# A decode block streaming its key and value cache: the query weights as four strided loads on two DMA queues

## The chip, the core and the metric

The kernel runs on one core of one Trainium2 chip. The metric is device time in microseconds (us) of one execution; lower is better. A core has five engines that run side by side, each with its own instruction queue: TensorE (PE) for matrix products, VectorE (DVE) and ScalarE (ACT) for elementwise work and reductions, GpSimd (POOL), and SyncE (SP), which here only issues transfers. Transfers between memory (HBM) and the on-chip SBUF of 128 partitions are done by 16 DMA engines. A transfer is issued by an engine into its own DMA queue: SyncE's transfers appear in the profile as queue q1, ScalarE's as queue q10. Engines and transfers wait for one another through semaphores.

## The reference, cut to what matters

One decoding step (a single new token for each of two sequences) of a transformer block, all in float32: layer norm, attention over a cache of 8192 keys and values for each of 32 heads of 128, and a gated feed-forward block, each with its residual.

```python
def _A_ref(x, k_cache, v_cache, wq, wo):       # x [2,1,512], caches [2,32,8192,128]
    q = (x @ wq).reshape(B, Sq, H, Dh).transpose(0, 2, 1, 3)
    scores = jnp.einsum("bhqd,bhkd->bhqk", q, k_cache) * (Dh ** -0.5)
    p = _softmax(scores, axis=-1)
    o = jnp.einsum("bhqk,bhkd->bhqd", p, v_cache)
    return o.transpose(0, 2, 1, 3).reshape(B, Sq, H * Dh) @ wo

h = x + _A_ref(_layernorm(x), k_cache, v_cache, wq, wo)     # wq [512,4096], wo [4096,512]
g, u = silu(_layernorm(h) @ w_gate), _layernorm(h) @ w_up   # [512,1792] each
out = h + (g * u) @ w_down                                  # w_down [1792,512]
```

The caches are by far the largest part of what is read: 2 x 268 MB of some 565 MB.

## The kernel before, in words

Everything is written out by hand: each engine has its own list of steps (`steps`), `do` appends an instruction that raises a semaphore, `wait` appends a wait for a semaphore to reach a value, and `emit` writes the lists out engine by engine.

**Units.** The attention is cut into U = 32 units, each of one sequence and two neighbouring heads. Keys of a unit fill one slot of 128 partitions by 64 KB (64 partitions per head, 128 keys of 128 numbers in each); there are two slots for keys, `kslot`, used in turn, and one, `vslot`, for values. For each unit VectorE multiplies the keys by the query (L435) and reduces the products to scores (L444), in two halves; TensorE and ScalarE make the softmax weights (L335 to L340, L395 to L401), and TensorE multiplies them with the values (`pe_values`, L345).

**Loads.** `loads` (L146 to L199) is a list in the order in which SyncE issues it (L594 to L597): wq first, then the first unit's keys in two halves, the second unit's keys, and from then on values and keys in turn, then wo, w_gate, w_up and w_down. `after` (L204 to L208) says which loads must wait because their slot is still in use: the first values wait for wq's last use, since wq lies in `vslot` until the query projection is done; the third unit's keys wait for the first unit's scores, and so on. wq, the halves of the first keys and the second unit's keys wait for nothing, so SyncE issues these four one behind another at the start.

Each whole load (wq, keys or values of a unit) is 8.389 MB: 128 rows of 64 KB, one for each partition. For wq a partition p holds the rows 4p to 4p+3 of the matrix, that is the four weights that belong to the features 4p to 4p+3 (L162).

**Start.** ScalarE issues the load of x (4 KB, L211). When it has landed, VectorE and GpSimd normalise it (`layernorm`, L235 to L258, called at L260), TensorE transposes the result (L255), and VectorE copies it into the form of a matmul operand (L289 and L294). TensorE then waits for that operand and for wq (L297) and makes the queries of all units: 8 groups of 16 instructions in the source, 128 matmuls in the trace (L308), each group copied out by ScalarE (L319). VectorE's first multiply waits for the first group's queries and for the first half of the first keys. The end of the last group is what frees `vslot` (`freed["wq", 0]`, L321).

Of the kernel before, what the change touches and what calls it, by code (L numbers as in the profile page):

```python
# [9 lines left out]
P = 128  # L10
# [3 lines left out]
class Program:  # L14
# [16 lines left out]
    def wait(self, engine, *points):  # L31
        for s, value in points:
            if self.known[engine].get(s, 0) < value:
                self.known[engine][s] = value
                self.steps[engine].append(lambda e, s=s, v=value: e.wait_ge(s, v))  # L35

    def do(self, engine, fn, sem=None, by=1):

        if sem is None:
            self.steps[engine].append(fn)  # L40
            return None
        self.count[sem] += by
        self.steps[engine].append(lambda e: fn(e).then_inc(sem, by))
        return sem, self.count[sem]
# [8 lines left out]
def decode_block(nc, x, k_cache, v_cache, wq, wo, w_gate, w_up, w_down, out):  # L53
# [24 lines left out]
    def sbuf(name, *shape, align=32):  # L78
        return nc.alloc_sbuf_tensor(name, list(shape), F32, align_bytes=align).ap()
# [7 lines left out]
    vslot = sbuf("vslot", P, SLOT, align=512)  # L87
# [44 lines left out]
    wait, do = g.wait, g.do  # L132
# [3 lines left out]
    s_dve_pe, s_act_pe, s_v = (g.sem(n) for n in ("dve_pe", "act_pe", "v"))  # L136
    s_k = [g.sem(f"k{n}") for n in range(2)]

    def alone(name):
        return g.sem(name)  # L140
# [3 lines left out]
    landed = {}  # L144
    freed = {}
    loads = []  # L146
# [7 lines left out]
    def load_kv(kind, i, parts=1):  # L154
        cache, t = (k_cache, kslot[i % 2]) if kind == "k" else (v_cache, vslot if i < U - 1 else v_last)
        n = SLOT // parts
        for c in range(parts):
            own = parts > 1 or (kind, i) == ("v", U - 1)
            sem = alone(f"{kind}{i}_{c}") if own else s_k[i % 2] if kind == "k" else s_v
            loads.append(((kind, i), c, t[:, c * n : (c + 1) * n], k_src(cache, i)[:, c * n : (c + 1) * n], sem))  # L160

    loads.append((("wq", 0), 0, vslot, wq.rearrange("(p c) m -> p (c m)", p=P), s_v))  # L162
    load_kv("k", 0, 2)
    for i in range(1, U):
        load_kv("k", i)
# [42 lines left out]
            after["k", i] = ("k", i - 2)  # L208


    do("scalar", lambda e: e.dma_start(xs, x.rearrange("b s d -> (b s) d")), x_in := alone("x"), 16)  # L211
    p0 = do("gpsimd", lambda e: e.memset(ident, 0.0), s_pool)
    wait("gpsimd", p0)
# [21 lines left out]
    def layernorm(src, ready):  # L235
        wait("vector", *ready)
        p = do("vector", lambda e: e.bn_stats(stats, src), s_dve)  # L237
        wait("vector", p)
        p = do("vector", lambda e: e.bn_aggr(mv, stats), s_dve)
        wait("vector", p)  # L240
        p = do("vector", lambda e: e.tensor_scalar(ve, mv[:, 1:2], EPS, None, op0=OP.add), s_dve)
        wait("gpsimd", p)
        p = do("gpsimd", lambda e: e.tensor_tensor(rstd, ve, mhalf, op=OP.pow), s_pool)
        wait("vector", p)
        p = do(
            "vector",
            lambda e: e.tensor_scalar(y, src, mv[:, 0:1], rstd, op0=OP.subtract, op1=OP.mult),
            s_dve,
        )
        normed = p  # L250
        wait("tensor", p, ident_done)
        for c in range(DC):
            p = do(
                "tensor",
                lambda e, c=c: e.transpose(yt[:, c, :], y.rearrange("b (p c) -> b c p", c=DC)[:, c, :], ident[:B, :B]),  # L255
                s_pe if c == DC - 1 else None,
            )
        return normed, p  # L258

    _, p = layernorm(xs, [(x_in, 16)])  # L260


    for t, value in (
# [25 lines left out]
    p = do("vector", lambda e: e.tensor_copy(xT, yt), s_dve)  # L289
    wait("vector", p)  # L290
    xb = osb.rearrange("p (c m) -> p c m", c=DC * B)
    xb_done = do(
        "vector",
        lambda e: e.tensor_copy(xb, xT.rearrange("p c b -> p (c b)")[:, :, None].to_broadcast([P, DC * B, HP])),  # L294
        s_dve,
    )
    wait("tensor", xb_done, landed[("wq", 0), 0])  # L297
    wqv = vslot.rearrange("p (c m k d) -> p c k m d", c=DC, k=2, d=DH)
    q_done = []
    for n, (m, b) in enumerate((m, b) for m in range(0, MQ, 4) for b in range(B)):  # L300
# [3 lines left out]
        for c in range(DC):  # L304
            for k in range(2):
                p = do(
                    "tensor",
                    lambda e, ps=ps, c=c, k=k, m=m, b=b: e.matmul(  # L308
                        ps[HALF[k]],
                        xb[:, c * B + b, :],  # L310
                        wqv[:, c, k, m : m + 4, :],
                        start=(c == 0),
                        stop=(c == DC - 1),
                    ),
# [111 lines left out]
    for i in range(U):  # L426
        m, b = divmod(i, B)
        parts = 2
        n = NJ // parts
        wait("vector", q_done[m // 4 * B + b])  # L430
        for c in range(parts):
# [7 lines left out]
            if i and c == 1:  # L439
                recip(i - 1)  # L440
            wait("vector", mult)
            p = do(
                "vector",
                lambda e, kt=kt, s=scores[i % 2][:, c * n : (c + 1) * n]: e.tensor_reduce(s, kt, axis=AX.X, op=OP.add),  # L444
                s_dve,
            )
        freed["k", i] = p
        if i:
# [16 lines left out]
    p = do(  # L465
        "vector",
        lambda e: e.tensor_tensor(
            om,
            oT.rearrange("p h b -> p b h")[:, :, :, None].to_broadcast([P, B, H, NQ]),
            quarter[:, None, None, :].to_broadcast([P, B, H, NQ]),  # L470
            op=OP.mult,
        ),
        s_dve,
    )
    wait("tensor", p)
    for b in range(B):
        p = do(
            "tensor",
            lambda e, b=b: e.matmul(
                oq_ps[:, b, :], om[:, b].rearrange("p h q -> p (h q)"), fold, start=True, stop=True  # L480
            ),
            s_pe if b == B - 1 else None,
        )
    wait("scalar", p)
    p = do("scalar", lambda e: e.activation(oq.rearrange("p c b -> p b c"), oq_ps, AF.Copy), s_act)
    wait("tensor", p, zeroed)
    for c in range(H):
        for e_, (c0, n) in enumerate(WO):
            if c0 == c:
                wait("tensor", landed[("wo", 0), e_])  # L490
        t = c % 4
        p = do(
            "tensor",
            lambda e, c=c, t=t: e.matmul(
                wide[0][32 * t : 32 * t + B, :],
                oq[:, c, :],
                wo_t[:, c * D : (c + 1) * D],
                start=(c < 4),
                stop=(c >= H - 4),
            ),  # L500
# [4 lines left out]
    p = do("scalar", lambda e: e.activation(osb, wide[0], AF.Copy), s_act)  # L505
# [13 lines left out]
    def project_f(first, ps):  # L519
        for c in range(DC):  # L520
            for e_, (c0, n) in enumerate(WF):
                if c0 == first + c:
                    wait("tensor", landed[("wf", 0), e_])
            w = wf_t[:, (first + c) * F : (first + c + 1) * F]
            for t in range(4):
                p = do(
                    "tensor",
                    lambda e, c=c, t=t, w=w: e.matmul(
                        ps[32 * t : 32 * t + 32, :],
                        hT[:, c, :],  # L530
                        w[:, t * FQ : (t + 1) * FQ],
                        start=(c == 0),
                        stop=(c == DC - 1),
                    ),
                    s_pe if c == DC - 1 and t == 3 else None,
                )
        return p

    gate, up = wide[1][:, :FQ], wide[0][:, :FQ]
    p = project_f(0, gate)  # L540

    wait("tensor", h1_done)
    for t in range(4):
# [8 lines left out]
    p = do("scalar", lambda e: e.activation(sg, gate, AF.Sigmoid), s_act)  # L552
    wait("vector", p)
    sg_done = do("vector", lambda e: e.tensor_mul(sg, gate, sg), s_dve)
    p = project_f(DC, up)
# [4 lines left out]
    p = do(  # L560
        "vector",
        lambda e: e.tensor_mul(
            gu.rearrange("p (c j) -> p j c", c=FB),
            up.rearrange("p (j c) -> p j c", c=FB),
            sg.rearrange("p (j c) -> p j c", c=FB),
        ),
        s_dve,
    )
    gT = rest[:, D + 2 * FQ : D + 3 * FQ]
    wait("vector", p)  # L570
    p = do("vector", lambda e: e.transpose(gT, gu), s_dve)
    wait("tensor", p)
    for c in range(FB):
# [3 lines left out]
        for t in range(4):  # L577
            p = do(
                "tensor",
                lambda e, c=c, t=t: e.matmul(  # L580
                    f_ps[32 * t : 32 * t + 32, :],
                    gT[:, c * 32 : (c + 1) * 32],
                    wd_t[:, c * D + t * P : c * D + (t + 1) * P],
                    start=False,
                    stop=(c == FB - 1),
                ),
# [62 lines left out]
```

## Time and profile before

| what | us |
|---|---|
| median of 3 runs (lowest, highest) | 1309.85 (1309.34, 1310.26) |
| the profiled execution, its own time | 1309.67 |
| its span, from the first instruction to the last | 1308.3 |
| VectorE busy | 1131.1 (86%) |
| TensorE's matmuls busy | 434.5 (33%) |
| DMA, mean over the span | 432 GB/s |

The times that the prediction works with are those of the one profiled execution, which also has some time around its span. The page of the profile gives busy times of each engine, a strip of 40 equal slices with the business of each engine in tenths, the DMA queues with their packets, and groups of instructions. The other views are the chain of work that ended last (followed back from the end, at each step to what released it), the timeline (instructions in order of time, with the idle time before each in square brackets and what ended it), the DMA view for a window (packets, queues, issues with the time from issue to landing) and busy times by window. An engine's name with a q (SPq, ACTq) marks an entry for issuing a transfer. L308 is line 308 of the kernel.

### The profile page before, as it was taken

Reading aid. Unit: us, or ns where it says so; the run is one execution under the profiler, and the core shown is the slowest. Engines: PE = TensorE matmul, PEld = TensorE weight load, DVE = VectorE, ACT = ScalarE, POOL = GpSimd, SP = SyncE. Lnnn points to the kernel's source line nnn. Section 1 sums busy time; section 2 is a strip of 40 time slices with the busy share of each in tenths; the row PEclk is TensorE's granted clock in tenths of the full one; section 3 lists DMA queues with packets and bytes.
Section 4 is the critical chain, followed back from the end, with each engine's and each line's share of the span. In section 5 each row is a group of like instructions: output and inputs, shape, how many; then the busy total and the mean of one; then the engine's idle time right before and its main releaser. Section 6 shows DMA issues by size and latency. Waiting matters only on the chain.

```text
span 1308.3 us, 6707 instructions
## 1 busy us (share of the span) xinstructions
PE 434.5 (33%) x2952; PEld 136.3 (10%) x2952; DVE 1131.1 (86%) x246; ACT 80.4 (6%) x271; POOL 3.1 (0%) x15
## 2 busy tenths in 40 slices
PE   3643223333213333312333321333332233332177
PEld 1210001011001011100101100101100010110022
DVE  0999988899888889988888988888998888898841
ACT  0100000000000000000000000000000000000010
POOL 0000000000000000000000000000000000000000
PEclk9865566666556666656666655666655666665578
DMA  9999999999999999999999999999999999999998
GB/s 404 443 433 439 427 433 435 437 431 439 427 443 423 445 421 445 431 437 437 431 439 427 443 423 445 421 443 431 439 437 427 443 427 439 427 441 425 441 424 371
DMA packets 10969, 564.79 MB, mean 432 GB/s; under 512 B 1222, under 2 KB 1230, under 8 KB 1616
## 3 DMA queue, kind: packets, MB, share of 16 engines
q1 hardware_dynamic: 10944, 564.66, 99.7%
q8 instruction: 5, 0.08, 0.0%
q14 instruction: 4, 0.03, 0.0%
q10 hardware_dynamic: 16, 0.01, 0.0%
HBM read 564.66 MB, written 0.00 MB: 432 GB/s over the span
## 4 chain that ended last, share of the span: by engine, by line
DMA 54%; DVE 45%; PE 1%; SPq 0%; issue 0%; DVEq 0%
DMA kslot<-in_A_k_cache_dram 48%; DVE kslot L435 22%; DVE s L444 22%; DMA kslot<-in_A_v_cache_dram 3%; DMA kslot<-in_B_w_down_dram 3%; PE opart L345 1%; DVE gm L388 0%; SPq L597 0%; DVE r L414 0%; PE bank L580 0%; DVE m L452 0%; DVE kslot L591 0%; DVEq L35 0%
## 5 line engine op out<-in xcount | busy, mean ns | idle before, releaser
L435 DVE TENSOR_TENSOR kslot<-kslot,qsb 128x8192 f32<-128x8192 f32 x64 | 555.6, 8681 | 127.7 <-DMA kslot<-in_A_k_cache_dram 127.7
L444 DVE TENSOR_REDUCE s<-kslot 128x64 f32<-128x8192 f32 x64 | 555.2, 8675 | 0.1
L345 PE MATMUL opart<-vslot,pz 128*8 128x512 f32 x1984 | 285.2, 740 | 246.0 <-DMA vslot<-in_A_v_cache_dram 246.0
L337 PE MATMUL bank<-gm,nscale 1*64 1x1 f32 x64 | 11.8, 250 | 358.4 <-DVE gm L388 358.4
L345 PEld LDWEIGHTS opart<-vslot,pz 128*8 128x8 f32 x1984 | 55.4, 103 | 449.7 <-DMA vslot<-in_A_v_cache_dram 248.7
L335 PE MATMUL bank<-ident,m 128*1 128x128 f32 x64 | 18.7, 395 | 169.3 <-DVE m L452 169.3
L337 PEld LDWEIGHTS bank<-gm,nscale 1*64 1x64 f32 x64 | 9.0, 199 | 374.4 <-DVE gm L388 374.4
L357 PE MATMUL bank<-rdiag,osb 128*128 128x2 f32 x256 | 34.5, 257 | 25.3 <-ACT osb L421 25.3
L395 ACT ACTIVATE nb<-bank 128x1 f32<-128x1 f32 x32 | 5.5, 171 | 552.8 <-PE bank L338 552.8
L416 ACT ACTIVATE rdiag<-fold,r 128x8 f32<-128x8 f32 x32 | 9.6, 301 | 484.5 <-DVE r L414 484.5
L357 PEld LDWEIGHTS bank<-rdiag,osb 128*128 128x128 f32 x256 | 31.8, 195 | 55.0 <-ACT osb L421 55.0
L308 PE MATMUL wide<-vslot,osb 128*64 128x512 f32 x128 | 29.3, 620 | 17.7 <-DMA vslot<-in_A_wq_dram 17.7
L340 PE MATMUL bank<-rs,sides 128*128 128x1 f32 x64 | 18.8, 363 | 41.5 <-ACT pz L401 41.5
L401 ACT ACTIVATE pz<-s,nb 64x128 f32<-64x128 f32 x64 | 25.5, 399 | 1.4
L421 ACT ACTIVATE osb<-opart 128x512 f32<-128x512 f32 x32 | 19.1, 597 | 70.5 <-PE opart L345 70.5
L335 PEld LDWEIGHTS bank<-ident,m 128*1 128x1 f32 x64 | 2.7, 81 | 172.8 <-DVE m L452 172.8
L340 PEld LDWEIGHTS bank<-rs,sides 128*128 128x128 f32 x64 | 16.1, 313 | 44.2 <-ACT pz L401 44.2
L308 PEld LDWEIGHTS wide<-vslot,osb 128*64 128x64 f32 x128 | 10.2, 143 | 36.0 <-issue 36.0
L237 DVE BATCH_NORM_STATS2 ln_stats<-attn 2x6 f32<-2x512 f32 x1 | 0.7, 686 | 12.9 <-PE attn L507 12.9
L401 ACT ACTIVATION_READ_ACCUMULATOR pz<-s,nb 64x1 f32 x64 | 11.8, 185 | 0.0
L338 PE MATMUL bank<-gm,nscale 1*64 1x1 f32 x64 | 11.8, 250 | 0.0
L452 DVE TENSOR_REDUCE m<-s 128x1 f32<-128x128 f32 x32 | 9.2, 286 | 1.1
(62 smaller groups left out, 96.1 us busy)
## 6 DMA issues: line engine op xcount, KB each, us to landing
kslot<-in_A_k_cache_dram SPq DMA_DIRECT2D x2, 4096.0 KB, 36.1
vslot<-in_A_wo_dram SPq DMA_DIRECT2D x1, 5120.0 KB, 22.5
kslot<-in_B_w_gate_dram SPq DMA_DIRECT2D x1, 3584.0 KB, 31.6
kslot<-in_B_w_up_dram SPq DMA_DIRECT2D x2, 1792.0 KB, 37.4
vslot<-in_A_wo_dram SPq DMA_DIRECT2D x1, 3072.0 KB, 29.4
kslot<-in_B_w_down_dram SPq DMA_DIRECT2D x2, 1024.0 KB, 30.4
kslot<-in_B_w_down_dram SPq DMA_DIRECT2D x1, 768.0 KB, 32.8
kslot<-in_B_w_down_dram SPq DMA_DIRECT2D x1, 512.0 KB, 33.6
```

Source lines behind the costliest of these rows:

```text
L308: lambda e, ps=ps, c=c, k=k, m=m, b=b: e.matmul(ps[HALF[k]], xb[:, c * B + b, :], wqv[:, c, k, m : m + 4, :], start=(c == 0), stop=(c == D ...
L335: e.matmul(mrow, m1, ident, start=True, stop=True).then_inc(s_pe, 1)
L337: e.matmul(nb_ps[HALF[0]], nscale, gm[:, 0:1], start=True, stop=True)
L338: e.matmul(nb_ps[HALF[1]], nscale, gm[:, 1:2], start=True, stop=True).then_inc(s_pe, 1)
L340: e.matmul(den, sides.rearrange("p w a -> p (w a)"), rs, start=True, stop=True).then_inc(s_pe, 1)
L345: inst = e.matmul(opart[32 * t : 32 * t + 2 * W, :], pz[:, w, :], t_v[:, w * W * DH : (w + 1) * W * DH], start=(w < 4), stop=(w >= NW - 4),)
L357: inst = e.matmul(ot_ps, osb[:, a * DH : (a + 1) * DH], rdiag[:, a::W], start=(a == 0), stop=(a == W - 1))
L401: lambda e, k=k, h=h: e.activation(pz[h, :, k * W : (k + 1) * W], s[h].rearrange("p (w a) -> p w a", a=W), AF.Exp, bias=nb[h], scale=SCALE ...
L416: do("scalar", lambda e: e.activation(rdiag, diag, AF.Copy, scale=r))
L421: do("scalar", lambda e: e.activation(osb, opart, AF.Copy), s_act_pe)
L435: mult = do("vector", lambda e, kt=kt, qb=qb: e.tensor_tensor(kt, kt, qb, op=OP.mult), s_dve)
L444: lambda e, kt=kt, s=scores[i % 2][:, c * n : (c + 1) * n]: e.tensor_reduce(s, kt, axis=AX.X, op=OP.add),
```

## The change

wq is no longer one load of 128 partitions issued by SyncE but four loads, each of some of the partitions: every 8th from 0 (16 rows), every 8th from 4 (16 rows), every 4th from 2 (32 rows) and every 2nd from 1 (64 rows). Together they hold each partition once. ScalarE issues the first three in front of x, each with a semaphore of its own; SyncE issues the fourth, first in its list as before. TensorE waits for all four landings ahead of the projection. What is loaded where, and all else, is as before.

```diff
-    loads.append((("wq", 0), 0, vslot, wq.rearrange("(p c) m -> p (c m)", p=P), s_v))
+    WQ = ((0, 8), (4, 8), (2, 4), (1, 2))
+    wq_rows = wq.rearrange("(p c) m -> p (c m)", p=P)
+    first, step = WQ[-1]
+    loads.append((("wq", 0), 0, vslot[first::step], wq_rows[first::step], s_v))
     load_kv("k", 0, 2)
...
+    wq_parts = [
+        do("scalar", lambda e, a=a, n=n: e.dma_start(vslot[a::n], wq_rows[a::n]), alone(f"wq{a}"), 16)
+        for a, n in WQ[:-1]
+    ]
     do("scalar", lambda e: e.dma_start(xs, x.rearrange("b s d -> (b s) d")), x_in := alone("x"), 16)
...
-    wait("tensor", xb_done, landed[("wq", 0), 0])
+    wait("tensor", xb_done, *wq_parts, landed[("wq", 0), 0])
```

## The prediction

> **What bounds the kernel now.** The page comes first: its span, its strip of DMA business and its queues.
>
> ```profile
> span 1308.3 us, 6707 instructions
> ...
> DMA  9999999999999999999999999999999999999998
> ...
> q1 hardware_dynamic: 10944, 564.66, 99.7%
> ```
>
> No slice of the strip is below nine tenths: the transfers fill the span, and nearly all of them are on q1, SyncE's queue. The next view is the chain of work that ended last, in order of time; three of its pieces, and its end:
>
> ```profile
> 1141.00 42.42 DMA kslot<-in_A_k_cache_dram
> ...
> 1218.26 42.43 DMA kslot<-in_A_v_cache_dram
> ...
> 1271.52 33.56 DMA kslot<-in_B_w_down_dram
> 1305.12 1.10 PE bank L580 x24
> 1306.24 0.29 DVE kslot L591
> ```
>
> The chain moves between VectorE and DMA, but the beat is that of DMA: from 1141.00 to 1218.26 are 77.26 us, in which the queue moves four whole loads of 8.389 MB, so 19.3 us for one, or 434 GB/s. The view of the DMA queues over 1100 us in the middle says the same, and gives the size of a packet:
>
> ```profile
> DMA packets 8184, 477.27 MB, mean 434 GB/s; under 512 B 898, under 2 KB 898, under 8 KB 898
> ```
>
> Of 8184 packets 898 are the tiny ones that raise semaphores; the other 7286 carry 477.27 MB, so 65.5 KB each: one partition's row of a whole load is one packet. 434 GB/s over 16 engines are 27.1 GB/s each, hence **2.41 us for a row** and 8 rows of each engine for a load (8 x 2.41 = 19.3). With 564.66 MB to move, 1300 us are gone at this rate; the span is 1308.3. Before and after the stream there are only some 8 us, and the stream itself has no hole that an edit of wq's load could fill. So a gain can come only from an earlier start, a loss only from a hole or from slower rows.
>
> **The start, where the change lies.** From the timeline (start, us, engine, line) of the first 82 us:
>
> ```profile
> 0.73 0.56 ACTq L211 DMA_DIRECT2D xs<-in_A_x_dram  x1
> 0.74 0.38 SPq L597 DMA_DIRECT2D vslot<-in_A_wq_dram  x1
> ...
> 1.17 1.55 SPq L597 DMA_DIRECT2D kslot<-in_A_k_cache_dram  x3
> ...
> 2.56 0.62 DVE L237 BATCH_NORM_STATS2 ln_stats<-xs 2x6 f32<-2x512 f32 x1
> ...
> 5.70 0.43 DVE L294 COPY osb<-xT 128x512 f32<-128x512 f32 x1
> ...
> 23.13 29.31 PE L308 MATMUL wide<-vslot,osb 128*64 128x512 f32 x128 [17.67 <-DMA vslot<-in_A_wq_dram]
> ...
> 28.45 0.60 ACT L319 ACTIVATE qsb<-wide 128x512 f32<-128x512 f32 x1 [25.84 <-PE wide L308]
> ...
> 32.75 8.70 DVE L435 TENSOR_TENSOR kslot<-kslot,qsb 128x8192 f32<-128x8192 f32 x1 [26.62 <-DMA kslot<-in_A_k_cache_dram]
> ...
> 52.48 0.33 SPq L597 DMA_DIRECT2D vslot<-in_A_v_cache_dram  x1
> ...
> 67.51 0.33 SPq L597 DMA_DIRECT2D kslot<-in_A_k_cache_dram  x1
> ...
> 81.98 9.96 PE L345 MATMUL opart<-vslot,pz 128*8 128x512 f32 x64 [3.08 <-DMA vslot<-in_A_v_cache_dram]
> ```
>
> The projection (L308) starts when wq has landed; the normalised x is ready at 5.70 + 0.43 = 6.13, 17 us too early to matter. The projection's end at 23.13 + 29.31 = 52.44 frees vslot, and SyncE issues the first v at 52.48. What that issue must not miss is the end of the loads in front of it (wq and the first two of k). Landing times, from the view of DMA over the first 5 us, and the packets of 50 to 60.4 us:
>
> ```profile
> vslot<-in_A_wq_dram SPq DMA_DIRECT2D x1, 22.3
> kslot<-in_A_k_cache_dram SPq DMA_DIRECT2D x1, 60.5
> ```
> ```profile
> DMA packets 66, 4.28 MB, mean 411 GB/s; under 512 B 0, under 2 KB 0, under 8 KB 0
> ```
>
> wq lands at 0.74 + 22.3 = 23.0. The whole k load, third of the three issues, lands about 62.6 (issued about 2.1). Until 60.4 no semaphore packet is seen, so no engine has finished that load. v lands by 81.98, 19.4 us behind the 62.6: a whole load's time, no hole.
>
> **The change, part by part.**
>
> *Bytes and rows.* Unchanged: 16 + 16 + 32 + 64 = 128 rows, as before. If they are dealt out evenly, an engine gets 1 + 1 + 2 rows on ScalarE's queue and 4 on SyncE's. At 2.41 us a row: 19.3 us, difference **0**. What k's first half waits for in line is the same sum of bytes, so it lands as before.
>
> *Start of the engines.* The first 2 us, in 40 slices of 0.05 us from 0.7:
>
> ```profile
> DMA  0000000000000000000299999009900909090900
> ```
>
> The first packets start in the slice at 1.65 (x) and 1.70, the last of the 16 rows in the slice at 2.55. A load of 16 rows asks for one row of each engine, so the engines could start closer together. All at 1.70 would be 0.85 us gained for the last; none closer, nothing. ScalarE now issues four DMAs by 0.38 to 0.56 us each (1.5 to 2.2 us in all) and has its table load behind them, but no work until 28.45, so this is hidden. A start later by one such issue would be the other end, +0.5. The first row gains most from a small load; I take **-0.2**.
>
> *x behind three loads on its queue.* This part moves a lot and should cost nothing. If an engine takes rows of the two queues in turn, x comes after ScalarE's four rows and three to five of SyncE's: between one row before wq's old landing and one row behind it, 20.6 to 25.4. From x to the ready operand it is 6.13 - 2.56 = 3.6 us. So the projection starts between 24.2 and 29.0, **1.1 to 5.9 us later**, and ends between 53.5 and 58.3. Three followers:
> - v's issue comes at 53.6 to 58.4. From an issue to its first row is 1.0 us (0.74 to 1.70), so rows are there at 54.6 to 59.4; the engines have k's rows until 60.4. Covered, by 1.0 us at the worst. Beyond, each further us would be a us at the end.
> - VectorE's first multiply needs the first q, at 28.45 + 0.60 = 29.05 before, now 30.2 to 35.0, against 32.75: 0 to 2.2 us late. VectorE's chain then frees the first k up to 2.2 us after 67.51, while v's rows run until 81.9. Covered by 12 us.
> - Behind the waiting matmul stands only PE's own work of the first unit, which needs VectorE's scores and v.
>
> So what is late next is v's issue, and it has cover: **0**.
>
> *The added waits.* PE waits for four landings instead of one. Three of them are past when the last row lands, and behind them nothing else stands on PE. 0.
>
> *Turns between two queues.* Before, an engine hardly ever changes queue, so its price isn't shown for data. The nearest row is an instruction fetch between two rows (43.8 to 44.9 us), and the page's sum for that queue:
>
> ```profile
> q8 instruction: 1, 0.02, 5.4%
> ```
> ```profile
> q8 instruction: 5, 0.08, 0.0%
> ```
>
> 5.4% of 16 engines' 1.1 us are 0.95 us for 16 KB, which at 27.1 GB/s are 0.60: 0.35 lost in one turn. Bounds: 0 to 8 x 0.35 = 2.8 us. This fetch comes alone to an idle queue; two queues that are both full have their next row waiting. I take **0**, and keep 2.8.
>
> *Rows with a step.* Every load in this trace is of 128 neighbouring rows; none shows what a row costs when the 16 engines write every 8th. Bounds: 2.41 us as in all 7286 rows, or twice that if two engines share a way in. All rows shown are at 2.41; I take that, and the other end is the main rival.
>
> **The sum:** 1309.67 (the profiled execution, 1.4 us more than its span) + 0 + 0 - 0.2 = 1309.5. That execution is 0.2 under the median 1309.85, so the forecast for the median is **1309.6 us**: no change. A measurement of this kernel tells about 0.2%, 2.6 us, from no change.
>
> **Rivals.**
>
> *Two rows meet on one way into SBUF (slower).* Whole loads run at 27.1 GB/s for each engine all through, so neighbouring rows are dealt out such that engines don't meet. With a step of 8 or 4 the same dealing may send two engines to one way in, no wider than one engine; then a row takes 4.8 us. If it holds for the two loads of 16 alone, 2 of 8 rows double: +4.8, 1314.5. If it holds for all four and the engines stay in step, 8 rows double: +19.3, 1329. wq then lands at 42 instead of 23, and everything behind moves along, since the stream has no slack to give it back. It passes 0.2% as soon as a little over one row of eight doubles. For it: the engines do start within a us of each other, so they are in step. Against it: no row in this trace is slow. I give the full form 0.31 and the smaller ones 0.17.
>
> [...]
>
> *Turns cost.* At 0.35 for each of 8 rows: +2.8, 1312.3; decides from 0.33 a row. Chance 0.06.
>
> *ScalarE's rows are served last.* If SyncE's queue went first, wq would land with k at 62.6, the projection would end at 62.6 + 3.6 + 29.3 = 95.5 and v's rows come at 96.5: a hole of 34 us, 1343. The tiny x got through beside the first rows (its statistics start at 2.56), which speaks against it. Chance 0.02.
>
> *A larger gain at the start.* All 0.85, 1308.9, is inside 0.2%; to pass 2.6 us more than the start would have to change. Chance 0.02.
>
> **How the numbers follow.** Forecast, gain included up to 0.85: 0.42; meeting rows 0.48; turns 0.06; service order 0.02; larger gain 0.02. Faster by over 0.2%: 0.02. Slower: 0.48 + 0.06 + 0.02 = 0.56. Within: 0.42. No change is the likeliest single outcome, with its own range 1308.8 to 1311, though the slower cases together weigh more. The range takes in the meeting rows to their full price: 1308.8 to 1330.
>
> **What would show it.** Right: q10 (ScalarE's) carries 4.2 MB and q1 that much less; the DMA strip of the first 25 us stays at 434 GB/s; L308 starts between 24 and 29; v's issue at 54 to 58; the beat in the chain stays 77.26; the end moves by under a us. Meeting rows: the windows between 2 and 40 us at half to three quarters of 434 GB/s, wq's last landing at 28 to 43, the later beat unchanged. Turns: the same dip, 3 us long. A late v: a hole at 60 us with rows at full speed on both sides. I am wrong if the first k load's landing moves by over 2.6 us, or if the stream has a hole that the rows above don't show.

## The result, and the profile after

The changed kernel takes 1318.32 us (median of 6 runs, 1318.04 to 1319.43) against 1309.76 for the first kernel in the same session (6 runs): 1.0067 of its time, 95% interval 1.0054 to 1.0079. It is **slower by 8.6 us**. The forecast was no change, 1309.6; the time lies inside the stated range, between the two prices of the main rival.

From the page of the changed kernel its span and its queue of ScalarE, and from its chain of waits two pieces four loads apart:

```profile
span 1317.1 us, 6711 instructions
...
q10 hardware_dynamic: 128, 4.20, 1.1%
```
```profile
1149.74 42.42 DMA kslot<-in_A_k_cache_dram
...
1227.00 42.43 DMA kslot<-in_A_v_cache_dram
```

Half of wq, 4.2 MB, now goes over q10, as intended. The beat of the stream is untouched: 1227.00 - 1149.74 = 77.26 us for four loads, to the hundredth what it was. So the loss is not spread over the run; it lies at the start. The table by windows of the changed kernel shows it (the last two columns are the busy share of the 16 DMA engines and GB/s; both count a packet where it starts, so a share can be over 1), followed by two of the same windows of the first kernel:

```profile
6.00:11.00 5.00, 0.00 (x0) 0.00 (x0) 0.00 (x0) 0.00 (x0) 0.00 (x0) 1.00 0.58 210
11.00:16.00 5.00, 0.00 (x0) 0.00 (x0) 0.00 (x0) 0.00 (x0) 0.00 (x0) 1.00 1.37 406
16.00:21.00 5.00, 0.00 (x0) 0.00 (x0) 0.00 (x0) 0.00 (x0) 0.00 (x0) 1.00 0.64 210
21.00:26.00 5.00, 0.00 (x0) 0.00 (x0) 0.00 (x0) 0.00 (x0) 0.00 (x0) 1.00 0.75 321
26.00:31.00 5.00, 0.00 (x0) 0.00 (x0) 0.00 (x0) 0.00 (x0) 0.00 (x0) 1.00 0.97 419
```
```profile
6.00:11.00 5.00, 0.00 (x0) 0.00 (x0) 0.12 (x1) 0.00 (x0) 0.00 (x0) 1.00 0.97 419
...
16.00:21.00 5.00, 0.00 (x0) 0.00 (x0) 0.00 (x0) 0.00 (x0) 0.00 (x0) 1.00 0.97 419
```

In two windows half as many rows start, 210 for 419 GB/s. The time of a row, below, is the surer measure. From 26 us the rate is whole again. A view of the DMA queues over 5 to 9.5 us tells whose rows these are:

```profile
DMA packets 17, 1.11 MB, mean 248 GB/s; under 512 B 0, under 2 KB 0, under 8 KB 0
## 3 DMA queue, kind: packets, MB, share of 16 engines
q10 hardware_dynamic: 16, 1.05, 104.5%
```

In the first slow stretch 16 packets of ScalarE's queue start, as many as there are engines: a load of every 8th partition. They would fill all 16 engines for 104.5% of these 4.5 us, so 4.7 us a row, where a row took 2.41. The second such load starts in the slow window from 16 to 21 us. The same view of other windows shows the two queues in turn: 16 rows of SyncE's queue start from 2 to 4.6 us, 16 of ScalarE's from 4.6 to 9.3, 16 of SyncE's from 9.3 to 12.

The timeline shows what that did behind (of the first kernel these lines are in the prediction):

```profile
0.73 2.14 ACTq L215 DMA_DIRECT2D vslot<-in_A_wq_dram  x3
...
33.52 0.68 DVE L244 BATCH_NORM_STATS2 ln_stats<-xs 2x6 f32<-2x512 f32 x1 [30.88 <-DMA xs<-in_A_x_dram]
...
37.21 29.23 PE L315 MATMUL wide<-vslot,osb 128*64 128x512 f32 x128 [0.72 <-DVE osb L301]
...
66.48 0.33 SPq L604 DMA_DIRECT2D vslot<-in_A_v_cache_dram  x1
...
90.79 9.10 PE L352 MATMUL opart<-vslot,pz 128*8 128x512 f32 x64 [1.55 <-DMA vslot<-in_A_v_cache_dram]
```

The projection is released by the normalised x, no longer by wq: the statistics of x start at 33.5 instead of 2.56, the projection starts at 37.21 instead of 23.13, and v is issued at 66.48 instead of 52.48. The first v lands by 90.79 instead of 81.98, 8.8 us later, and the end is later by the same amount. A window around v's issue in the changed kernel:

```profile
62.00:66.00 4.00, 4.00 (x22) 1.24 (x18) 4.00 (x1) 0.60 (x1) 0.00 (x0) 1.00 0.83 360
66.00:70.00 4.00, 0.44 (x4) 0.00 (x0) 3.97 (x2) 0.60 (x1) 0.00 (x0) 1.00 0.83 283
```

Over these 8 us the mean is 322 GB/s. The same two windows of the first kernel, counted by starts too, have 508 and 311, 410 in the mean, and the stream runs at 434: by that some 1.7 to 2.1 us are lost here, an estimate. A view of the DMA queues over 64.6 to 67.4 us shows where:

```profile
q1 hardware_dynamic: 15, 0.07, 5.7%
q8 instruction: 1, 0.02, 2.1%
```

In these 2.8 us one row (0.07 MB) starts, where each of the 16 engines starts one every 2.41 us in the stream; the other 14 packets are the tiny ones, and the one of q8 is an instruction fetch. Rows of 2.41 us that started before 64.6 are done by 67.0, so most engines then have nothing to move. The 16 rows of v that start next, by 70.4 us, take 3.1 us each (103.4% of 3 us). That is the hole which the forecast had held to be covered.

Two theories for the slow rows were put to the test: that two engines **meet** on one way into SBUF when a load writes every 8th partition, and that **turns** between two queues cost time. A third question was what the **late x** adds.

### The profile page after: what moved, and what is told of

Its sections match the earlier page's. It is cut to its first block, busy times and chain, and to the rows that moved or that the text cites. A ratio compares the mean times of both kernels' runs of the same rounds, so it can differ in the third digit from the quotient of the medians.

```text
span 1317.1 us, 6711 instructions
## 1 busy us (share of the span) xinstructions
PE 432.5 (33%) x2952; PEld 134.7 (10%) x2952; DVE 1131.3 (86%) x246; ACT 80.3 (6%) x271; POOL 3.1 (0%) x15
## 4 chain that ended last, share of the span: by engine, by line
DMA 53%; DVE 45%; PE 1%; ACTq 0%; issue 0%; SPq 0%; ACT 0%; POOL 0%; DVEq 0%
DMA kslot<-in_A_k_cache_dram 45%; DVE kslot L442 22%; DVE s L451 22%; DMA kslot<-in_A_v_cache_dram 3%; DMA kslot<-in_B_w_down_dram 3%; DMA xs<-in_A_x_dram 2%; PE opart L352 1%; PE wide L315 0%; DVE gm L395 0%; ACTq L215 0%; DVE r L421 0%; SPq L604 0%; PE bank L587 0%; DVE ln_stats L244 0%; PE bank L262 0%
## 5 line engine op out<-in xcount | busy, mean ns | idle before, releaser
L342 PEld LDWEIGHTS bank<-ident,m 128*1 128x1 f32 x64 | 2.7, 81 | 170.1 <-DVE m L459 170.1
```

Source lines behind the costliest of these rows:

```text
L342: e.matmul(mrow, m1, ident, start=True, stop=True).then_inc(s_pe, 1)
```

## The experiments

Unless said otherwise a diff is against the changed kernel. Each median is set beside the first kernel's in the same session: 1309.72 for every 4th, all four in one queue, neighbouring partitions and x in front of the three loads; 1309.83 for the other four.

### Every 4th instead of twice every 8th

```diff
-    WQ = ((0, 8), (4, 8), (2, 4), (1, 2))
+    WQ = ((0, 4), (2, 4), (1, 2))
```

> The two loads of every 8th partition are one load of every 4th (32 rows); ScalarE's queue still has 64 rows in front of x. Meeting theory (two engines share one way into SBUF when only every 8th partition is written): no row doubles, wq lands by 24 us, the projection starts at 26 to 30, the first v is issued before 60 and there is no hole; the end is 0 to 1 us behind the first kernel, 1309.8 to 1311. Turns theory (a row costs more when the engines change queue): four rows still alternate with SyncE's, so the rows stay slow and the end is at 1316 to 1319.

Measured: 1311.08 us (10 runs), ratio 1.0011 (1.0001 to 1.0020). Its windows and timeline:

```profile
6.00:11.00 5.00, 0.00 (x0) 0.00 (x0) 0.00 (x0) 0.00 (x0) 0.00 (x0) 1.00 0.97 419
```
```profile
30.02 29.55 PE L315 MATMUL wide<-vslot,osb 128*64 128x512 f32 x128 [0.72 <-DVE osb L301]
...
59.61 0.33 SPq L604 DMA_DIRECT2D vslot<-in_A_v_cache_dram  x1
```

The same 32 partitions in one load instead of two, still on the second queue and still side by side with SyncE's load (landing 18.9 and 19.8 us after their issue): 419 GB/s in each window from 6 to 21 us, and 7.2 of 8.6 us are gone. Turns aren't the cause of the slow rows. The projection still starts late, at 30.0, and v's issue at 59.61 is just not early enough; what that costs is told apart below.

### All four loads in one queue

```diff
-    loads.append((("wq", 0), 0, vslot[first::step], wq_rows[first::step], s_v))
+    for i, (first, step) in enumerate(WQ):
+        sem = s_v if i == len(WQ) - 1 else alone(f"wq{first}")
+        loads.append((("wq", 0), i, vslot[first::step], wq_rows[first::step], sem))
...
```

All of WQ stands in SyncE's list, in order; ScalarE's list holds x alone.

> All four loads of wq are issued by SyncE, in the same order; ScalarE issues x alone, at once. Meeting theory: the two loads of 16 rows still take twice as long, 2 x 2.4 us more, wq lands at 28, the projection starts there because x is early, v is issued at 57 to 58 before k's end at 65, no hole; the end is 4.8 us behind the first kernel, 1314.6. Turns theory: no alternation, no loss, 1309.8.

Measured: 1314.54 us (5 runs), ratio 1.0037 (1.0022 to 1.0051), where 1314.6 was expected of meeting rows and 1309.8 of turns.

```profile
2.00:6.00 4.00, 0.64 (x4) 0.55 (x4) 2.40 (x8) 0.62 (x1) 1.63 (x6) 1.00 1.21 262
6.00:11.00 5.00, 0.00 (x0) 0.00 (x0) 0.12 (x1) 0.00 (x0) 0.00 (x0) 1.00 0.99 210
11.00:16.00 5.00, 0.00 (x0) 0.00 (x0) 0.00 (x0) 0.00 (x0) 0.00 (x0) 1.00 1.05 419
```
```profile
27.95 29.61 PE L312 MATMUL wide<-vslot,osb 128*64 128x512 f32 x128 [22.49 <-DMA vslot<-in_A_wq_dram]
...
57.58 0.33 SPq L601 DMA_DIRECT2D vslot<-in_A_v_cache_dram  x1
```

With no second queue and x early, the two loads of 16 are slow one behind the other: half rate in the windows until 11 us, whole rate from there. wq releases the projection 4.8 us later than in the first kernel, and the end is 4.8 us later: some 2.4 us for each load of 16 rows with a step of 8. Up to 0.3 us of the 4.8 may not be the slow rows: the kernel of every 4th in one queue, below, has none and is 0.3 us behind the first kernel, though that is within what can be told.

### Four loads of every 8th partition

```diff
-    WQ = ((0, 8), (4, 8), (2, 4), (1, 2))       # in the kernel of one queue
+    WQ = ((0, 8), (4, 8), (2, 8), (6, 8), (1, 2))
```

> SyncE issues wq in five loads: four of every 8th partition (from 0, 4, 2 and 6) and one of every 2nd from 1; ScalarE issues x alone. Meeting theory: twice as many doubled rows as in e2_one_queue, 4 x 2.4 us more, end 9.7 to 10.1 us behind the first kernel, 1319.5. A price for each load, whatever its rows: one load more than e2, 1315 to 1316.

Measured: 1319.39 us (4 runs), ratio 1.0074 (1.0058 to 1.0089); 9.6 us more than the first kernel, twice the 4.8 of two such loads.

```profile
6.00:11.00 5.00, 0.00 (x0) 0.00 (x0) 0.13 (x1) 0.00 (x0) 0.00 (x0) 1.00 0.99 210
...
16.00:21.00 5.00, 0.00 (x0) 0.00 (x0) 0.00 (x0) 0.00 (x0) 0.00 (x0) 1.00 0.99 210
21.00:26.00 5.00, 0.00 (x0) 0.00 (x0) 0.00 (x0) 0.00 (x0) 0.00 (x0) 1.00 1.06 419
```

The price goes with the doubled rows, not with the number of loads: a price for each load would have given 1315 to 1316.

### Every 4th in one queue

```diff
-    WQ = ((0, 8), (4, 8), (2, 4), (1, 2))       # in the kernel of one queue
+    WQ = ((0, 4), (2, 4), (1, 2))
```

> SyncE issues wq in three loads: every 4th, every 4th from 2, every 2nd from 1; ScalarE issues x alone. Meeting theory: no doubled row, no alternation, no late x; only the first row comes 0.3 to 0.4 us later, since a load with a step takes longer to issue: 1310.0 to 1310.2. If every load with a step is slow: 1314 or more.

Measured: 1310.14 us (11 runs), ratio 1.0003 (0.9994 to 1.0012): no difference that can be told. The rate is 419 GB/s in each window from 6 to 21 us, where two of them have 210 in the changed kernel. A step as such is not slow; the step of 8 is.

### Neighbouring partitions

```diff
-    WQ = ((0, 8), (4, 8), (2, 4), (1, 2))
+    WQ = ((0, 16), (16, 32), (32, 64), (64, 128))     # slices first:last, no step
```

> The changed kernel with the same four sizes, but of neighbouring partitions: 0 to 15, 16 to 31, 32 to 63, 64 to 127. [...] Turns theory: the order of queues is as in the changed kernel, so 1318.

Measured: 1340.17 us in a single run, 30 us more than the first kernel, where the theory of turns gives 1318.

```profile
q10 hardware_dynamic: 16, 1.05, 170.1%
```
```profile
6.00:11.00 5.00, 0.00 (x0) 0.00 (x0) 0.00 (x0) 0.00 (x0) 0.00 (x0) 1.00 0.84 157
11.00:16.00 5.00, 0.00 (x0) 0.00 (x0) 0.00 (x0) 0.00 (x0) 0.00 (x0) 1.00 0.46 92
...
31.00:36.00 5.00, 0.00 (x0) 0.00 (x0) 0.00 (x0) 0.00 (x0) 0.00 (x0) 1.00 1.03 210
36.00:41.00 5.00, 0.00 (x0) 0.00 (x0) 0.00 (x0) 0.00 (x0) 0.00 (x0) 1.00 0.99 210
```

The sizes and the order of issue are those of the changed kernel; only the partition numbers differ, and the loss is more than three times as large. The first line is of the view over 0 to 5 us: the 16 rows of the first block of 16 neighbours take 8.5 us each (170.1% of 5 us), 3.5 times 2.41, and in the windows the rate falls to 92 GB/s, near a quarter. With blocks of 32 and 64 neighbours it is a half, 210. So what counts is which partitions a load holds. The same slice is taken of wq in HBM and of the SBUF tile, here and in all the runs, so the runs don't tell apart where the rows are read and where they are written.

### x in front of the three loads

```diff
+    do("scalar", lambda e: e.dma_start(xs, x.rearrange("b s d -> (b s) d")), x_in := alone("x"), 16)
     wq_parts = [
...
-    do("scalar", lambda e: e.dma_start(xs, x.rearrange("b s d -> (b s) d")), x_in := alone("x"), 16)
```

> The changed kernel with x issued ahead of the three loads on ScalarE's queue. Both theories keep the slow rows. If the late x makes a hole of its own at 67 us: the projection starts when wq lands, at 31 to 32, v is issued at 61, the hole goes, and the end is 1.5 to 3 us earlier than the changed kernel, 1315.3 to 1316.8. If the late x is covered: 1318.3 as the changed kernel.

Measured: 1315.55 us (4 runs), ratio 1.0044 (1.0028 to 1.0061): 2.8 us less than the changed kernel.

```profile
6.00:11.00 5.00, 0.00 (x0) 0.00 (x0) 0.12 (x1) 0.00 (x0) 0.00 (x0) 1.00 0.91 210
```
```profile
32.02 30.67 PE L315 MATMUL wide<-vslot,osb 128*64 128x512 f32 x128 [26.56 <-DMA vslot<-in_A_wq_dram]
...
62.72 0.33 SPq L604 DMA_DIRECT2D vslot<-in_A_v_cache_dram  x1
...
87.57 9.57 PE L352 MATMUL opart<-vslot,pz 128*8 128x512 f32 x64 [2.09 <-DMA vslot<-in_A_v_cache_dram]
```

The slow rows stay, but wq itself releases the projection again, v is issued 3.8 us earlier, and v lands 3.2 us earlier than in the changed kernel. So the late x has a price of its own, on top of the slow rows.

### Every 4th with x in front

```diff
-    WQ = ((0, 8), (4, 8), (2, 4), (1, 2))       # in the kernel with x in front
+    WQ = ((0, 4), (2, 4), (1, 2))
```

> As e1_every4th (every 4th, every 4th from 2, every 2nd from 1), with x issued ahead of the two on ScalarE's queue. Late-x theory (what e1 has lost beside a start that is 0.3 us later is v's late issue): the projection starts at 23 to 24, v's issue has 7 us of cover again, and the end is 0.3 to 0.6 us behind the first kernel, 1310.0 to 1310.3. If alternating queues have a price of their own: still 1311.

Measured: 1310.07 us (11 runs), ratio 1.0002 (0.9993 to 1.0011). The kernel of every 4th lost 1.4 us against the first kernel of its session, this one 0.2, which is no difference that can be told: moving x alone took the rest of the loss. Two queues that carry wq side by side (its loads land 20.1 us after their issue on one and 17.5 on the other), with x early and no doubled row, cost nothing: 1310.07 here and 1310.14 in one queue.

### One whole load on ScalarE's queue

Against the first kernel: wq stays one load of 128 partitions, issued by ScalarE in front of x.

```diff
-    loads.append((("wq", 0), 0, vslot, wq.rearrange("(p c) m -> p (c m)", p=P), s_v))
+    wq_in = do("scalar", lambda e: e.dma_start(vslot, wq.rearrange("(p c) m -> p (c m)", p=P)), s_v, 16)
     do("scalar", lambda e: e.dma_start(xs, x.rearrange("b s d -> (b s) d")), x_in := alone("x"), 16)
...
-    wait("tensor", xb_done, landed[("wq", 0), 0])
+    wait("tensor", xb_done, wq_in)
```

> No step at all: wq is one load of 128 partitions as in the first kernel, but ScalarE issues it in front of x, while SyncE issues only k. Late-x theory: wq's 8 rows alternate with k's half rows and land at 31 to 32, x behind them at 33 to 34, the projection starts at 37 and ends at 66 to 67, v's rows come at 67 to 68, but k's rows end at 60.5 as before: a hole of 6 to 8 us at full speed on both sides, end at 1316 to 1318. If the slow rows were the whole loss: 1309.8 to 1310.5.

Measured: 1319.14 us (4 runs), ratio 1.0070 (1.0054 to 1.0085), 1.1 us above the range expected of the late x, and far from what slow rows alone would give.

```profile
vslot<-in_A_wq_dram ACTq DMA_DIRECT2D x1, 31.5
```
```profile
38.11 30.33 PE L308 MATMUL wide<-vslot,osb 128*64 128x512 f32 x128 [0.72 <-DVE osb L294]
...
68.48 0.33 SPq L597 DMA_DIRECT2D vslot<-in_A_v_cache_dram  x1
```
```profile
11.00:16.00 5.00, 0.00 (x0) 0.00 (x0) 0.00 (x0) 0.00 (x0) 0.00 (x0) 1.00 0.97 419
...
61.00:66.00 5.00, 5.00 (x26) 1.66 (x24) 5.00 (x2) 1.19 (x2) 0.00 (x0) 1.00 0.02 3
```

Here the rows run at the whole rate, and yet 9.3 us are lost, because wq shares the engines with k and lands at 32, x behind it, and the projection ends at 68.4. From 61 to 66 us the queue moves 3 GB/s: it is empty, waiting for v's issue. This is the hole of the changed kernel in its pure form.

## Why the prediction was wrong

**What bounds the kernel, and the beat.** Right. The stream has no slack; in the kernel of one queue, 4.8 us lost before 16 us were still there at the end, and in the changed kernel the beat did not move.

**Bytes and rows dealt out evenly, 0.** Right: q10 carries 4.2 MB, and every 4th in one or two queues runs at the whole rate, 419 GB/s.

**Start of the engines, -0.2.** Wrong in sign, small. The first rows come later, not earlier (below).

**Rows with a step, "2.41 us as in all 7286 rows".** This is the step that failed. Two of an engine's eight rows took nearly twice as long, 4.7 us in the changed kernel and 4.9 in the kernel of one queue. The view had no load of fewer than 128 neighbouring rows in it, so "no row in this trace is slow" said nothing on the question, and the nearest row was taken for an answer. The rival's smaller form, the two loads of 16 alone, had the price right: +4.8, 1314.5 forecast, 1314.54 measured with the loads in one queue. That it fits to some hundredths is luck, since up to 0.3 of the 4.8 us may be something else. Its full form did not come: the loads of 32 and 64 rows with steps of 4 and 2 run at the whole rate (419 GB/s in each window from 11 to 31 us in the kernel of one queue).

The runs show the rates, and that they go with the partition numbers: every 8th partition at half rate (210 of 419 GB/s), 16 neighbours at 8.5 us a row instead of 2.41, 32 or 64 neighbours at half rate (210), every 4th or every 2nd at the whole (419). What sets them no run shows; that engines meet on one way into SBUF is the author's supposition.

**x behind three loads, "covered, by 1.0 us at the worst".** Failed as well. The bounds for x, 20.6 to 25.4, were worked out with rows of 2.41 us; with the doubled rows in front of it x was there only at 33.5 and the projection started 14 us later, not 1.1 to 5.9. The cover was thin even without them: in the kernel of every 4th the projection started at 30.0, past its bound of 29.0, v was issued at 59.61 instead of the 58.4 at the worst, and moving x gave 1.0 us. A hidden step was costed on its own, and the other edit of the same change used up its cover.

**VectorE's chain.** Its first multiply came 10 us late (43.08 for 32.75), not up to 2.2, but the third k load's issue, 77.84 for 67.51, was still ahead of v's landing at 90.79. Covered, as said.

**Turns.** Right with 0 for normal rows (1310.07 in two queues, 1310.14 in one).

**The sum as the runs give it:** slow rows 4.8 (one queue, against the first kernel), the same rows with two queues 1.0 more (1315.55 - 1314.54), late x 2.8 (1318.32 - 1315.55): 8.6.

The middle term is small: the two intervals overlap, though each of the four runs with two queues is above each of the five with one. The traces give a reason for about half of it. An engine's row right behind a doubled one is slow too. In the kernel of one queue the doubled loads stand together, so this happens once (first line, the view over 11 to 14 us); with two queues and x in front they stand apart, and it happens twice (second line, 11.5 to 14.5; third, 22 to 23.2, half rows of k). The other 16 packets of the first and third line are tiny.

```profile
q1 hardware_dynamic: 32, 1.05, 94.5%
```
```profile
q1 hardware_dynamic: 16, 1.05, 95.8%
```
```profile
q1 hardware_dynamic: 32, 0.52, 130.8%
```

94.5% of 3 us are 2.8 us for a row that takes 2.4 elsewhere, 95.8% are 2.9, and 130.8% of 1.2 us are nearly 1.6 for a half row that takes 1.2. With the other views of this kind, the slow rows of an engine take 4.85, 4.92 and 2.82 us in one queue, which is 5.3 more than usual rows; with two queues 3.10 (the first row of all, which in one queue is a doubled one), 4.54, 2.87, 4.72 and a half row of 1.56, which is 5.9 more. That gives 0.6 of the 1.0, an estimate, and the two profiled executions (1314.36 and 1314.99) differ by as much. Why a row behind a doubled one is slow, no run shows. Within the 2.8, the empty time, the slow first rows of v and the instruction fetch that falls into the same stretch were not separated.

None of the versions tried is faster than the first kernel; the two that come nearest differ from it by no more than can be measured.

## What to carry to other kernels

A load's rate depended here on which partitions it holds, and how far they reach is not the measure: every 8th of 128 ran at half rate (210 of 419 GB/s), every 4th and every 2nd at the whole (419). So a load should be cut into pieces of a kind that a run has shown at the whole rate, or along the free dimension, as the first unit's keys are (their halves run at 419 GB/s in the first kernel, 26 to 31 us). Ask this before pricing a piece by the rate of the whole. What stood behind a load on its queue got that load's time (the statistics of x started at 33.5 us behind the three loads, at 2.56 in front of them), and a small operand that releases something large belongs in front. When a step is called covered, work out its cover with the bad end of the change's other steps, not with the good one.

## What the runs showed of the hardware that was not expected

A load of some of the partitions took longer to issue than a whole one. The one issue of wq by SyncE took 0.38 us in the first kernel. The five stepped issues of the kernel with four loads of 16, and the three of every 4th in one queue:

```profile
0.74 3.15 SPq L601 DMA_DIRECT2D vslot<-in_A_wq_dram  x5
```
```profile
0.74 1.83 SPq L601 DMA_DIRECT2D vslot<-in_A_wq_dram  x3
```

That is 0.6 us each. The step is a part of it, but not all. In the kernel of neighbouring partitions ScalarE's three issues took 0.45 us each instead of 0.71 in the changed kernel (1.36 and 2.14 for three), while SyncE's one issue of 64 neighbours took 0.57, as long as its stepped one:

```profile
0.73 1.36 ACTq L215 DMA_DIRECT2D vslot<-in_A_wq_dram  x3
0.74 0.57 SPq L604 DMA_DIRECT2D vslot<-in_A_wq_dram  x1
```

The first rows come later too. In the changed kernel's strip of the first 5 us (40 slices of 0.125 us) they start in the slice at 2.0, where the first kernel's started at 1.70. All 16 packets that start in these 5 us are of SyncE's queue, so its load of 64 rows came first, not a load of 16:

```profile
DMA  0000000000000000999999900000000000000000
...
q1 hardware_dynamic: 16, 1.05, 62.1%
```

In the kernel of one queue a load of 16 does come first, and its first rows start in the slice at 2.12 (the one at 1.62 is x):

```profile
DMA  0000000000000200099099090000000000000000
```

So a small first load did not bring the engines to work sooner here; it brought them 0.4 us later.
